# Sinkhorn gate steps, first-gate scaling and slice-pair combinations placed differently in the expert stage of one kernel

## The chip, the cores and the metric

The kernel runs on one core of a Trainium2 chip. The metric is the device time of one execution in microseconds (us). Every time below comes from runs on the chip or from one profiled execution.

## What is computed

The reference is clustered attention, then a squared-relu MLP, then a layer of eight experts whose gates are balanced by Sinkhorn iterations. Only the last part bears on the change. `x` has 1536 tokens of 512 features, `E` is 8, each expert has 1024 hidden features:

```
logits = x @ w_gate
logits = logits - logits.max()
P = exp(logits)
for _ in range(8):
    P /= P.sum(1, keepdims=True) + 1e-09      # rows: one sum per token
    P /= P.sum(0, keepdims=True) + 1e-09      # columns: one sum per expert
    P *= N / E
out = 0
for e in range(E):
    out += P[:, e:e+1] * (relu(x @ w1[e]) @ w2[e])
```

## The kernel before

**The work of the expert stage.** Tokens lie in four slices of 384 (`x1[0]` to `x1[3]`), taken as two slice pairs (0, 1) and (2, 3). The function `blocks` (line 875) runs 64 blocks, n = 0 to 63: for each slice pair the 32 weight units in turn (four units for each expert). A block multiplies x by one unit of the first expert weights in Winograd's form: seven products instead of eight, each a group of six matmuls into one PSUM tile (lines 949, 962, 976, 985, all recorded at the helper's line 120). In the text products are named by the left operand: 0, 4, 1, 5, 3, 2, 6, which is their order on TensorE. Three of them (0, 1, 6) have plain halves of x as right operand (`xh`, `xl`), the other four the combinations T1 to T4 of the two slices of the pair (`th`, `tl`). All float32 data are held in two parts.

**What stands between the products.** VectorE adds the products up (lines 952, 963, 964, 977, 978, 979, 986; ScalarE copies product 0 at line 951), relu leaves a high part `hh` on ScalarE (line 901) and a low part `hl` on VectorE (line 902), and TensorE applies the second expert weights to the relu results of the block before (`second`, line 922: nine matmuls at a time, four times per block). Each expert's result is gathered in PSUM for four blocks and then added to the output with its gate (`drain`, lines 932 and 934). ScalarE and GpSimd meanwhile split the weights of the next block in four quarters (`pieces`, lines 828 to 842), and a DMA fetches the raw unit three blocks ahead (line 807).

**PSUM.** The products of a block take turns in two PSUM buffers named `t` (`ps`, line 108, with `lanes` set to 2). A product can start when the product, or whatever else was given a buffer, two turns earlier has been read for the last time.

**The order of work** is the program's order on each engine, written out by hand; nothing is moved by a scheduler. A step that `blocks` calls between two products stands at that place in the queues of all engines that it uses.

**The gate.** `gate_steps` (line 706) makes ten steps, and with the logits of the last slice and their transposition there are twelve. From block 1 on, the helper `more` (line 939) pops one of them at two places of each block: ahead of product 3, and at the block's end. So they run in blocks 1 to 6. `gmax1` and `gmax2` find the largest logit and take the exponential; `gmax2` goes on with the first `rows`. Each `cols` step then has a matmul with a matrix of ones (line 737) that gives the column sums, four small VectorE instructions (739 to 742), a multiplication of `pm` (743), and `rows`: three small instructions (729 to 731) and another multiplication of `pm` (732). The small vectors `cs` and `rs` lie in SBUF; the PSUM tile of the matmul is last read at line 739.

**The first gate.** Expert 0's sum is drained in block 4, before the gate is known, and copied without a factor (line 932). At the end of block 6 six VectorE instructions (line 1002) scale it.

**The turn.** Block 31 is the last of the first slice pair. There, VectorE forms the T combinations of the second pair (`combine`, lines 849 to 861, ten instructions on operands in SBUF), and `parts` splits them in two (line 872 on ScalarE, 873 on GpSimd) before block 32 needs them.

Of the kernel before, what the change touches and what calls it, by code (L numbers as in the profile page):

```python
# [17 lines left out]
P = 128  # L18
# [20 lines left out]
# Per group of four heads: shifts of its preparation steps against their places.  # L39
# [14 lines left out]
class Kernel:  # L54
    """Clustered attention, a squared-relu MLP and Sinkhorn-gated experts.

    A float32 matrix product is carried by three float32r passes over the parts
    x = hi + lo, where hi is x rounded to 12 significant bits and lo the exact rest.
    """
# [7 lines left out]
    def build(self):  # L67
        tc = self.tc
        with ExitStack() as ctx:
# [7 lines left out]
            # The space of what prepares the heads goes to the first weights when it is done.  # L77
# [23 lines left out]
    def experts_follow(self):  # L101
        """The space of the first stage's weights goes to the second's."""
        self.top.__exit__(None, None, None)
        self.right.__exit__(None, None, None)
        self.right = self.tc.tile_pool(name="late", bufs=1, side="right", reuse_waits="tile")
        self.late = self.right.__enter__()
        self.top = self.tc.tile_pool(name="top2", bufs=1, reuse_waits="tile")
        self.upper = self.top.__enter__()
# [7 lines left out]
    def mm3(self, out, pairs):  # L116
        """out = sum of products of (stationary, moving) pairs."""
        n = len(pairs)
        for i, (a, b) in enumerate(pairs):
            self.nc.tensor.matmul(out, a, b, start=(i == 0), stop=(i == n - 1))  # L120

# [1 line left out]

    def constants(self):
        nc, per = self.nc, self.per
        cst = per.tile([P, 2 * P + 1], F32, name="cst")
        nc.sync.dma_start(cst, self.cst_in)
        self.ident, self.floor = cst[:, :P], cst[:, 2 * P : 2 * P + 1]
        # Its values, like the 0/1 it is multiplied with, are exact in bfloat16.
        self.band = per.tile([P, P], BF16, name="band")  # L130
        nc.vector.tensor_copy(self.band, cst[:, P : 2 * P])
# [13 lines left out]
    def centroids(self, craw):  # L145
        """Normalised centroids, transposed to [(j, d), (head, c)], as the zero-padded
        stationaries of each quadrant."""
# [10 lines left out]
        # Partition (hp, j, c) keeps its columns of half j only.  # L158
# [20 lines left out]

    def norms(self, n, soon=False):  # L180
        """Steps that give 1 / (|x| + 1e-6) for the rows of q and k."""
# [43 lines left out]
    def prepare(self, n, soon=False):  # L225
        """Steps, each with its place, that load four heads, assign clusters and build their
        stacked operands."""
# [113 lines left out]
    def attention(self):  # L341
# [123 lines left out]
        def values(half, part):  # L465
            """A third of the half head's product with v."""
# [82 lines left out]

    def load_unit(self, u):  # L550
        """Weight unit u of the first stage, in float64 words."""
# [5 lines left out]
    def words(self, u, part=None):  # L557
        """float64 to float32, first part: the high word's exponent is rebiased by a scaling, the
        low word becomes a multiple of its last bit's weight."""
# [11 lines left out]
    def bits(self, u, part=None):  # L571
        """Second part: t has the sign, the exponent and 20 fraction bits, a the power of two."""
# [9 lines left out]
    def join(self, u):  # L582
        """Third part: the low word's share is added."""
# [18 lines left out]
    def experts(self):  # L602
        nc = self.nc
        # A group of weight units is applied to each chunk of tokens in turn.
# [101 lines left out]
        def gate_steps():  # L706
            lg, pm = self.lg, self.pm
            n_t = NCH * TT
            flat = pm.rearrange("p t e -> p (t e)")

# [8 lines left out]
            def gmax2():  # L719
# [5 lines left out]
                rows()  # L725

            def rows():
                rs = self.tile("rs", [P, n_t])
# [5 lines left out]
            def cols(last):  # L734
                def run():
                    ps = self.ps("t", [P, n_t, NE])
                    nc.tensor.matmul(ps.rearrange("p t e -> p (t e)"), self.ones, flat, start=True, stop=True)
                    cs = self.tile("cs", [P, NE])
                    nc.vector.reduce_sum(cs, ps.rearrange("p t e -> p e t"), axis=AX.X)
                    nc.vector.tensor_scalar_add(cs, cs, 1e-9)  # L740
                    nc.vector.reciprocal(cs, cs)
                    nc.vector.tensor_scalar_mul(cs, cs, float(NT // NE))
                    nc.vector.tensor_tensor(pm, pm, cs.unsqueeze(1).to_broadcast([P, n_t, NE]), op=ALU.mult)
                    if not last:
                        rows()
                return run

            return [gmax1, gmax2] + [cols(i == 7) for i in range(8)]

        # The step after which each unit is split: its slot is free and its use ahead.  # L750
# [18 lines left out]
        for d, *st in (  # L769
# [3 lines left out]
            (10, self.combine, 1, 0, 0, 1), (11, self.parts, 1, 0, 1), (11, self.combine, 2, 0, 0, 1),  # L773
            (12, self.parts, 2, 0, 1), (12, self.combine, 0, 0, 0), (13, self.parts, 0, 0),
            (14, self.combine, 0, 0, 1), (14, self.combine, 3, 0, 0), (15, self.parts, 3, 0), (15, self.parts, 0, 1),
            (15, self.combine, 3, 0, 1),
# [13 lines left out]
        extra = [(logits, NCH - 1), (turn_logits, NCH - 1)] + [(st,) for st in gate_steps()]  # L790
        self.blocks(lambda i: second(n_steps - 2 + i), extra)

# [1 line left out]
    #  # L794
    # relu(x w1) is formed for two chunks of tokens and two blocks of hidden features at a time.
    # With A the blocks of w1' (hidden features by halves of the contraction) and B those of x'
    # (halves of the contraction by chunks), Winograd's form needs seven products:
    #   S1 = A21 + A22, S2 = S1 - A11, S3 = A11 - A21, S4 = A12 - S2
    #   T1 = B12 - B11, T2 = B22 - T1, T3 = B22 - B12, T4 = T2 - B21
    #   P1 = A11 B11, P2 = A12 B21, P3 = S4 B22, P4 = A22 T4, P5 = S1 T1, P6 = S2 T2, P7 = S3 T3  # L800
    #   C11 = P1 + P2, U = P1 + P6, V = U + P7, C12 = U + P5 + P3, C21 = V - P4, C22 = V + P5

    def fetch(self, k):
        """Unit k of the experts' weights: [A11 A12 A22 A21 | w2 of both blocks]."""
# [4 lines left out]
    def pieces(self, k, i):  # L809
        """The quarters of splitting unit k into A11 A12 A22 S1 S2 S3 S4 and w2."""  # L810
# [34 lines left out]
    def combine(self, i, sp, *js):  # L845
        """Halves js of T_i of slice pair sp (0 for T4)."""
        nc = self.nc
        x0, x1 = self.x1[2 * sp], self.x1[2 * sp + 1]
        sub = lambda o, a, b: nc.vector.tensor_tensor(o, a, b, op=ALU.subtract)  # L849
        for j in js:  # L850
            t = self.tile("r", [P, CH], bufs=4) if sp else self.tile("c", [P, CH], bufs=4, pool=self.late)
            self.cv[i, j] = t
# [4 lines left out]
            else:  # L857
# [3 lines left out]
                if i == 0:  # L861
                    sub(t, t, x0[:, 2 + j])

# [11 lines left out]
    def blocks(self, before, extra):  # L875
# [7 lines left out]
        def product(n, a, b):  # L883
            """a-th left operand times b, a chunk's half (c, half) or T_b."""
# [54 lines left out]
        def more():  # L939
            if extra:  # L940
                st = extra.pop(0)
                st[0](*st[1:])

        self.parts(3, 1)
        for n in range(N2):
# [12 lines left out]
            if turn:  # L958
                self.combine(2, 1, 0, 1)
                self.combine(0, 1, 0, 1)  # L960
                self.parts(2, 0, 1)
            ta, tb = product(n, 1, (c0, 1)), product(n, 5, 3)
# [8 lines left out]
            if turn:  # L971
                self.combine(3, 1, 0, 1)
                self.parts(3, 0, 1)
            if n > 0:
                more()
# [7 lines left out]
            if n > 0:  # L983
                self.pieces(n + 1, 2)
            ta = product(n, 6, (c1, 1))
# [3 lines left out]
            if turn:  # L989
                self.parts(0, 0, 1)  # L990
                self.combine(1, 1, 0, 1)
                self.parts(1, 0, 1)
            self.pieces(n + 1, 3)
            self.fetch(n + 3)
            if n > 0:
                more()
            if n == 2 * FP - 2:
                assert not extra
                for t in range(2):
                    for m in range(TT):  # L1000
                        p = self.pm[:, t * TT + m, :1]
                        nc.vector.tensor_scalar_mul(acc[t][:, m], acc[t][:, m], p)
# [10 lines left out]
def _constants():  # L1013
    """Identity; the matrix that finds the first of equal maxima; a row's floor; 1/2.

    The rows of a quadrant are (j, cluster); quadrants hold the q and k of a head pair. From the
    0/1 marks of the maxima the matrix gives 1 (k: BIG) for the first of a group and 0 or less
    for all else.
    """
# [9 lines left out]
def _layouts(inputs):  # L1029
    q, k, v = inputs["q"], inputs["k"], inputs["v"]  # L1030
    qk = np.stack([q, k])
    # [X, b, t, pair, j, s, d] -> [b, t, (pair, X), (j, d), s]
# [10 lines left out]
    # An expert's w1 [(half, kt, p), (block, fp, f)] as [fp][p][(block, half), (kt, f)], w2 [(block, fp, p), m]  # L1043
    # as [fp][p][block, m].
# [24 lines left out]
```

## Time and profile before

| | |
|---|---|
| Median of 3 timed runs | 1633.49 us (1632.96 to 1636.36) |
| Span of the profiled execution, first to last instruction | 1629.9 us |
| Own device time of the profiled execution | not listed apart; the median is 3.6 us over its span |
| TensorE busy | 1555.6 us (95%) |
| VectorE, ScalarE, GpSimd busy | 1069.4, 762.6, 888.3 us |
| Mean granted TensorE clock | 0.985 of full speed |

TensorE's matmuls are pipelined, so its busy share says only that matmuls were in flight. The stage of the experts takes the span from some 585 us to the end.

### The profile page before, as it was taken

The numbers are of one execution on the slowest core, as the hardware profiler recorded it, in microseconds if no ns is written. First come the engines' busy times: TensorE is split into PE (matmuls) and PEld (weight loads), VectorE is DVE, ScalarE is ACT, GpSimd is POOL, SyncE is SP. The second block draws the span as 40 slices with busy tenths as digits, with TensorE's granted clock in tenths as the row PEclk, the third lists the DMA queues.
The fourth block names the chain that finished last, engine by engine and source line by source line (L and its number), as shares of the span: only waits on it lengthen the run. The fifth ranks groups of instructions, "written<-read, shape, count | busy, mean of one in ns | idle before, by whom it ended". The sixth has DMA issues, their size and how long they took to land.

```text
span 1629.9 us, 21771 instructions
## 1 busy us (share of the span) xinstructions
PE 1555.6 (95%) x8136; PEld 1408.9 (86%) x8136; DVE 1069.4 (66%) x1610; ACT 762.6 (47%) x1426; POOL 888.3 (54%) x650
## 2 busy tenths in 40 slices
PE   4899998799999999989999999998999999999998
PEld 4878987699999988778989888887898898888887
DVE  7999989787887665765555555557455555555554
ACT  4789898566565643323333333333343333333331
POOL 5665337332323564546566565667566565665652
PEclk7999999899999999999999999999999999999999
DMA  9774452021111011112112121222121121211211
GB/s 269 177 189 105 88 146 79 26 74 56 55 49 52 1 52 52 52 52 78 60 70 78 52 78 53 77 78 91 52 78 69 62 78 52 78 65 65 78 53 39
DMA packets 26793, 124.69 MB, mean 77 GB/s; under 512 B 4448, under 2 KB 4576, under 8 KB 16448
## 3 DMA queue, kind: packets, MB, share of 16 engines
q1 hardware_dynamic: 26112, 120.95, 22.7%
q0 software_dynamic: 576, 2.36, 0.6%
q8 instruction: 64, 1.05, 0.3%
q14 instruction: 41, 0.34, 0.1%
HBM read 99.80 MB, written 3.15 MB: 63 GB/s over the span
## 4 chain that ended last, share of the span: by engine, by line
PE 78%; DVE 14%; ACT 4%; issue 2%; POOL 1%; DMA 1%; SPq 0%; DVEq 0%; ACTq 0%; POOLq 0%
PE t L120 31%; PE s L922 21%; PE y L922 10%; PE s L664 6%; PE pv L473 2%; PE u L120 2%; DVE atl L463 2%; PE s L422 2%; DVE m L428 2%; PE t L450 1%; DVE sums L480 1%; ACT e L435 1%; DVE hl L650 1%; DVE c L849 1%; ACT ath L457 1%
## 5 line engine op out<-in xcount | busy, mean ns | idle before, releaser
L901 ACT ACTIVATE hh<-c 128x384 fp32r<-128x384 f32 x256 | 134.5, 525 | 638.9 <-PE y L922 241.7
L902 DVE SCALAR_TENSOR_TENSOR hl<-c,hh 128x384 fp32r<-128x384 f32 x256 | 247.9, 970 | 177.3 <-ACT hh L901 177.2
L842 POOL TENSOR_TENSOR wl<-raw,wh 128x1024 fp32r<-128x1024 f32 x64 | 154.0, 2407 | 375.5 <-ACT wh L841 375.5
L922 PE MATMUL s<-wh,hh 128*128 128x512 f32 x512 | 204.7, 400 | 0.0
L922 PE MATMUL s<-wl,hh 128*128 128x512 f32 x512 | 203.6, 398 | 0.0
L922 PE MATMUL s<-wh,hl 128*128 128x512 f32 x512 | 203.0, 396 | 0.0
L120 PE MATMUL t<-th,ah 128*128 128x384 f32 x512 | 174.2, 340 | 10.6 <-DVE c L952 7.0
L834 POOL TENSOR_TENSOR al<-sm,ah 128x1024 fp32r<-128x1024 f32 x64 | 171.7, 2683 | 9.6 <-ACT ah L831 9.6
L120 PE MATMUL t<-th,al 128*128 128x384 f32 x512 | 173.4, 339 | 0.0
L120 PE MATMUL t<-tl,ah 128*128 128x384 f32 x512 | 172.9, 338 | 0.0
L120 PE MATMUL t<-xh,ah 128*128 128x384 f32 x384 | 130.7, 340 | 6.0 <-DVE c L978 3.6
L120 PE MATMUL t<-xh,al 128*128 128x384 f32 x384 | 129.7, 338 | 0.0
L120 PE MATMUL t<-xl,ah 128*128 128x384 f32 x384 | 129.4, 337 | 0.0
L963 DVE TENSOR_TENSOR c<-t,c 128x384 f32<-128x384 f32 x64 | 35.7, 557 | 136.3 <-PE t L120 136.0
L587 POOL TENSOR_TENSOR fa<-fa,wraw 128x1024 f32<-128x1024 f32 x16 | 39.1, 2445 | 150.9 <-ACT r L646 107.9
L832 POOL TENSOR_TENSOR al<-raw,ah 128x768 fp32r<-128x768 f32 x64 | 118.8, 1856 | 0.0
L922 PEld LDWEIGHTS s<-wh,hl 128*128 128x128 f32 x512 | 97.2, 190 | 24.2
L120 PEld LDWEIGHTS t<-th,ah 128*128 128x128 f32 x512 | 96.5, 189 | 16.8 <-DVE c L952 7.9
L922 PEld LDWEIGHTS s<-wh,hh 128*128 128x128 f32 x512 | 97.0, 189 | 12.0
L922 PEld LDWEIGHTS s<-wl,hh 128*128 128x128 f32 x512 | 96.9, 189 | 12.0
L922 PE MATMUL y<-wh,hl 128*128 128x512 f32 x256 | 100.9, 394 | 0.0
L922 PE MATMUL y<-wl,hh 128*128 128x512 f32 x256 | 100.9, 394 | 0.0
(218 smaller groups left out, 4093.6 us busy)
## 6 DMA issues: line engine op xcount, KB each, us to landing
raw<-in_w SPq DMA_DIRECT2D x64, 1024.0 KB, 4.8
wraw<-in_w SPq DMA_DIRECT2D x16, 1024.0 KB, 4.8
raw<-in_qk SPq DMA_DIRECT2D x16, 384.0 KB, 4.2
ka<-hi SPq DMA_DIRECT2D x28, 192.0 KB, 3.7
nat<-in_qkn SPq DMA_DIRECT2D x6, 768.0 KB, 5.2
vraw<-in_v SPq DMA_DIRECT2D x8, 384.0 KB, 4.5
out<-x SPq DMA_DIRECT2D x12, 256.0 KB, 2.1
qa<-hi SPq DMA_DIRECT2D x14, 192.0 KB, 2.6
```

Source lines behind the costliest of these rows:

```text
L120: self.nc.tensor.matmul(out, a, b, start=(i == 0), stop=(i == n - 1))
L422: nc.tensor.matmul(s[:, u, :HALF], a[:, qs], k[:, u * HALF : u * HALF + HALF], start=(a is qa), stop=(a is qb))
L428: nc.vector.tensor_reduce(m, sc[g][:, :, :HALF], axis=AX.XY, op=ALU.max, negate=True)
L587: nc.gpsimd.tensor_tensor(a, a, raw[:, :, 0].bitcast(F32), op=ALU.mult)
L664: nc.tensor.matmul(o, a, b, start=(start and i == 0), stop=(stop and i == 2))
L832: nc.gpsimd.tensor_tensor(al[:, : 3 * Q], raw[:, : 3 * Q], f32(ah[:, : 3 * Q]), op=ALU.subtract)
L834: nc.gpsimd.tensor_tensor(al[:, 3 * Q :], self.sums.rearrange("p a b -> p (a b)"), f32(ah[:, 3 * Q :]), op=ALU.subtract)
L842: nc.gpsimd.tensor_tensor(wl, raw[:, 1024:], f32(wh), op=ALU.subtract)
L901: nc.scalar.activation(hh, c, AF.Relu)
L902: nc.vector.scalar_tensor_tensor(hl, c, 0.0, f32(hh), op0=ALU.max, op1=ALU.subtract)
L922: nc.tensor.matmul(ys[t][m], a, b, start=(start and i == 0), stop=(stop and i == 2))
L963: nc.vector.tensor_tensor(p1, ta, p1, op=ALU.add)
```

## The change

Three edits, all in the expert stage.

1. The Sinkhorn steps. `rows` and `total` (the old `cols`) are now 16 single steps; with the logits, their transposition, `gmax1` and `gmax2` there are 20. `more` is called at four places of a block instead of two (ahead of product 1, of product 3, of product 6, and at the end), so the steps run in blocks 1 to 5. The vectors `rs` and `cs` lie in PSUM, `rs` in a `t` buffer of its own and `cs` beside the column sums in theirs. One instruction is left out per column step: the addition and the multiplication by the constant are one.
2. The first-gate scaling is six multiplications on ScalarE instead of VectorE, two at each of the first three places of block 7.
3. The combinations of the second slice pair are eight VectorE instructions instead of ten, each reading two operands in SBUF, one at each place of blocks 29 and 30; T1 and T4 overwrite parts of `x1` in place. Block 31 keeps only the splitting, T1's ahead of product 6.

```diff
         def gate_steps():
...
-                rows()
+
+            def total():
+                ps = hold["ps"] = self.ps("t", [P, n_t + 1, NE])
+                nc.tensor.matmul(
+                    ps[:, :n_t].rearrange("p t e -> p (t e)"), self.ones, flat, start=True, stop=True
+                )
+                cs = ps[:, n_t]
+                nc.vector.reduce_sum(cs, ps[:, :n_t].rearrange("p t e -> p e t"), axis=AX.X)
+                nc.vector.tensor_scalar(cs, cs, 1e-9, float(NE / NT), op0=ALU.add, op1=ALU.mult)
+                nc.vector.reciprocal(cs, cs)
+                nc.vector.tensor_tensor(pm, pm, cs.unsqueeze(1).to_broadcast([P, n_t, NE]), op=ALU.mult)
 
             def rows():
-                rs = self.tile("rs", [P, n_t])
+                rs = self.ps("t", [P, n_t])
...
-            def cols(last):
...
-            return [gmax1, gmax2] + [cols(i == 7) for i in range(8)]
+            def first_gate(t, m):
+                a = self.flat[t].rearrange("p (m n) -> p m n", n=512)[:, m]
+                nc.scalar.mul(a, a, pm[:, t * TT + m, :1])
+
+            steps = [(gmax1,), (gmax2,)] + [(rows,), (total,)] * 8
+            return steps, [(first_gate, t, m) for t in range(2) for m in range(TT)]
...
+    def next_combine(self, i, j):
+        nc = self.nc
+        x0, x1 = self.x1[2], self.x1[3]
+        t = {1: x1[:, j], 0: x0[:, 2 + j]}.get(i)
+        if t is None:
+            t = self.tile("r", [P, CH], bufs=4)
+        self.cv[i, j] = t
+        a, b, op = {
+            3: (x1[:, 2 + j], x1[:, j], ALU.subtract), 2: (self.cv.get((3, j)), x0[:, j], ALU.add),
+            1: (x1[:, j], x0[:, j], ALU.subtract), 0: (self.cv.get((2, j)), x0[:, 2 + j], ALU.subtract),
+        }[i]
+        nc.vector.tensor_tensor(t, a, b, op=op)
...
-        def more():
-            if extra:
+        ahead = [(self.next_combine, i, j) for i in (3, 2, 1, 0) for j in range(2)]
+
+        def more(n):
+            if 0 < n < U2 and extra:
                 st = extra.pop(0)
+                st[0](*st[1:])
+            elif n == 2 * FP - 1 and scales:
+                for st in scales[:2]:
+                    st[0](*st[1:])
+                del scales[:2]
+            elif U2 - 3 <= n < U2 and ahead:
+                st = ahead.pop(0)
                 st[0](*st[1:])
...
             if turn:
-                self.combine(2, 1, 0, 1)
-                self.combine(0, 1, 0, 1)
                 self.parts(2, 0, 1)
+            more(n)
             ta, tb = product(n, 1, (c0, 1)), product(n, 5, 3)
...
             if turn:
-                self.combine(3, 1, 0, 1)
                 self.parts(3, 0, 1)
-            if n > 0:
-                more()
+            more(n)
             ta, tb = product(n, 3, 1), product(n, 2, 0)
...
+            if turn:
+                self.parts(1, 0, 1)
+            more(n)
             ta = product(n, 6, (c1, 1))
...
             if turn:
                 self.parts(0, 0, 1)
-                self.combine(1, 1, 0, 1)
-                self.parts(1, 0, 1)
             self.pieces(n + 1, 3)
             self.fetch(n + 3)
-            if n > 0:
-                more()
-            if n == 2 * FP - 2:
-                assert not extra
-                for t in range(2):
-                    for m in range(TT):
-                        p = self.pm[:, t * TT + m, :1]
-                        nc.vector.tensor_scalar_mul(acc[t][:, m], acc[t][:, m], p)
+            more(n)
```

## Rows read from the trace of the kernel before

**Rows 1.** The page's head and its part 1, busy time by engine.

```profile
span 1629.9 us, 21771 instructions
...
PE 1555.6 (95%) x8136; PEld 1408.9 (86%) x8136; DVE 1069.4 (66%) x1610; ACT 762.6 (47%) x1426; POOL 888.3 (54%) x650
```

**Rows 2.** Busy time by stretch; bounds are starts of a block's first product.

```profile
core 0: us, PE busy (x) PEld busy (x) DVE busy (x) ACT busy (x) POOL busy (x), PEclk, DMA share, GB/s
597.37:615.85 18.48, 17.69 (x91) 14.83 (x90) 7.99 (x14) 6.11 (x11) 10.79 (x8) 1.00 0.16 58
615.85:632.68 16.83, 16.46 (x83) 14.25 (x81) 7.60 (x14) 5.36 (x10) 9.71 (x7) 1.00 0.15 62
597.37:730.17 132.80, 121.01 (x578) 104.13 (x577) 85.05 (x162) 40.68 (x71) 68.75 (x50) 0.96 0.15 56
706.63:730.17 23.54, 18.55 (x82) 15.98 (x80) 16.37 (x22) 5.10 (x9) 9.86 (x7) 0.85 0.12 45
730.17:1091.56 361.39, 361.39 (x1795) 324.39 (x1794) 197.23 (x289) 121.83 (x207) 223.49 (x161) 1.00 0.18 68
1091.56:1130.16 38.60, 34.02 (x158) 29.27 (x156) 29.17 (x35) 14.29 (x26) 29.58 (x22) 0.96 0.20 76
```

**Rows 3.** Waits of TensorE from 600 to 720 us: total, times, longest.

```profile
PE t L120 <- DVE c L952: 7.0, 3, 5.0
PE t L120 <- DVE c L978: 3.6, 3, 1.8
```

**Rows 4.** Single lines: duration in ns (least, median, most), first and last start, shape.

```profile
L742 DVE TENSOR_SCALAR cs<-cs x8: 171/1129/2305, 644.0 to 708.3; 128x8 f32<-128x8 f32 x8
...
L1002 DVE TENSOR_SCALAR x<-x,pm x6: 474/942/2018, 711.4 to 716.3; 128x512 f32<-128x512 f32 x6
...
L963 DVE TENSOR_TENSOR c<-t,c x64: 543/557/559, 590.9 to 1607.0; 128x384 f32<-128x384 f32 x64
...
L739 DVE TENSOR_REDUCE cs<-t x8: 249/255/258, 641.6 to 707.5; 128x8 f32<-128x96 f32 x8
...
L729 DVE TENSOR_REDUCE rs<-pm x8: 252/253/253, 634.2 to 701.2; 128x12 f32<-128x96 f32 x8
...
L737 PEld LDWEIGHTS t<-pm,ones x16: 187/188/189, 641.0 to 706.5; 128*128 128x128 f32 x16
```

**Rows 5.** Timeline over the end of block 4 and the start of block 5.

```profile
668.74 0.35 PE L737 MATMUL t<-pm,ones 128*128 128x96 f32 x2
...
668.87 0.42 PE L120 MATMUL t<-xh,ah 128*128 128x384 f32 x1
...
669.79 0.25 DVE L739 TENSOR_REDUCE cs<-t 128x8 f32<-128x96 f32 x1
...
670.18 0.42 PE L120 MATMUL t<-th,ah 128*128 128x384 f32 x1
...
671.77 0.26 DVE L732 TENSOR_TENSOR pm<-pm,rs 128x96 f32<-128x96 f32 x1
```

**Rows 6.** Timeline of block 1 where product 6 starts.

```profile
612.35 0.33 PE L120 MATMUL t<-xh,ah 128*128 128x384 f32 x1
...
612.88 0.56 DVE L902 SCALAR_TENSOR_TENSOR hl<-c,hh 128x384 fp32r<-128x384 f32 x1 [1.39 <-ACT hh L901]
```

**Rows 7.** Timeline of block 30, VectorE and GpSimd after product 5.

```profile
1082.83 2.20 DVE L902 SCALAR_TENSOR_TENSOR hl<-c,hh 128x384 fp32r<-128x384 f32 x1
...
1084.58 2.72 POOL L834 TENSOR_TENSOR al<-sm,ah 128x1024 fp32r<-128x1024 f32 x1
1085.51 0.56 DVE L977 TENSOR_TENSOR c<-t,c 128x384 f32<-128x384 f32 x1 [0.48 <-PE t L120]
```

**Rows 8.** Timeline across the end of block 31 and the start of block 32.

```profile
1112.28 4.54 POOL L873 TENSOR_TENSOR tl<-r,th 128x384 fp32r<-128x384 f32 x4 [2.01 <-ACT th L872]
1112.31 2.70 DVE L849 TENSOR_TENSOR r<-x,x 128x384 f32<-128x384 f32 x2
...
1116.49 0.47 ACT L951 COPY c<-t 128x384 f32<-128x384 f32 x1
...
1117.02 0.45 PE L120 MATMUL t<-xh,ah 128*128 128x384 f32 x1 [2.30 <-ACT c L951]
```

**Rows 9.** Line 932, ScalarE's scaled copies of 128x512.

```profile
L932 ACT ACTIVATE x<-s,pm x4: 668/679/687, 1185.2 to 1194.0; 128x512 f32<-128x512 f32 x4
```

More of the change, by code (lines that the diff above doesn't have):

```diff
@@ L709, in gate_steps @@
             flat = pm.rearrange("p t e -> p (t e)")
+            hold = {}
             def gmax1():
@@ L732, in rows @@
                 nc.vector.tensor_tensor(pm, pm, rs.unsqueeze(2).to_broadcast([P, n_t, NE]), op=ALU.mult)
-            def cols(last):
[L735 to L746, printed above, removed]
-            return [gmax1, gmax2] + [cols(i == 7) for i in range(8)]
+            def first_gate(t, m):
[3 more added lines that the diff above has]
+            return steps, [(first_gate, t, m) for t in range(2) for m in range(TT)]
         plan = {}
@@ L772, in experts @@
             (10, pieces, 1, 2), (14, pieces, 0, 3), (15, self.fetch, 2),
[L773 to L776, printed above, removed]
+            (10, self.combine, 1, 0, 1), (11, self.parts, 1, 0, 1), (11, self.combine, 2, 0, 1),
+            (12, self.parts, 2, 0, 1), (12, self.combine, 0, 0), (13, self.parts, 0, 0),
+            (14, self.combine, 0, 1), (14, self.combine, 3, 0), (15, self.parts, 3, 0), (15, self.parts, 0, 1),
+            (15, self.combine, 3, 1),
         ):
@@ L789, in experts @@
                 st[0](*st[1:])
-        extra = [(logits, NCH - 1), (turn_logits, NCH - 1)] + [(st,) for st in gate_steps()]
-        self.blocks(lambda i: second(n_steps - 2 + i), extra)
+        gates, scales = gate_steps()
+        self.blocks(lambda i: second(n_steps - 2 + i), [(logits, NCH - 1), (turn_logits, NCH - 1)] + gates, scales)
     def fetch(self, k):
@@ L843, in pieces, with combine @@
             self.raws.pop(U1 + k)
-    def combine(self, i, sp, *js):
+    def combine(self, i, *js):
         nc = self.nc
-        x0, x1 = self.x1[2 * sp], self.x1[2 * sp + 1]
+        x0, x1 = self.x1[0], self.x1[1]
         sub = lambda o, a, b: nc.vector.tensor_tensor(o, a, b, op=ALU.subtract)
         for j in js:
-            t = self.tile("r", [P, CH], bufs=4) if sp else self.tile("c", [P, CH], bufs=4, pool=self.late)
-            self.cv[i, j] = t
+            t = self.cv[i, j] = self.tile("c", [P, CH], bufs=4, pool=self.late)
             if i == 1:
@@ L873, in parts, with blocks @@
             nc.gpsimd.tensor_tensor(tl[:, i, j], t, f32(th[:, i, j]), op=ALU.subtract)
-    def blocks(self, before, extra):
+    def blocks(self, before, extra, scales):
         nc = self.nc
@@ L990, in blocks @@
                 self.parts(0, 0, 1)
-                self.combine(1, 1, 0, 1)
-                self.parts(1, 0, 1)
             self.pieces(n + 1, 3)
             self.fetch(n + 3)
-            if n > 0:
-                more()
-            if n == 2 * FP - 2:
-                assert not extra
-                for t in range(2):
-                    for m in range(TT):
-                        p = self.pm[:, t * TT + m, :1]
-                        nc.vector.tensor_scalar_mul(acc[t][:, m], acc[t][:, m], p)
+            more(n)
+            assert n < 2 * FP or not extra + scales
         second(N2 - 1, 0, 0)
```

## The prediction

> **What bounds the kernel now.** I began with the page's engine shares: TensorE is busy for 1555.6 of 1629.9 us, 95% [rows 1]. That says where the bound is, not where time is lost, so next I cut the expert stage into stretches at the starts of its blocks. The 23 blocks from 730.17 to 1091.56 take 361.39 us, TensorE busy in all of it, at full granted clock: 15.71 us per block [rows 2]. No small edit on another engine can shorten these. Two stretches are longer than their blocks. Blocks 1 to 7, which hold the gate, take 132.80 us, 22.8 more than 7 x 15.71. Blocks 31 and 32, the turn, take 38.60, 7.2 more than 2 x 15.71 [rows 2]. These 30.0 us are all that the three edits can reach.
>
> Then I asked who keeps TensorE waiting in the gate stretch: VectorE's additions at lines 952 and 978, 10.6 us in six waits [rows 3]. They aren't slow; line 963, an addition of the same kind, takes 557 ns whatever else runs [rows 4]. They stand behind gate instructions in VectorE's queue, and some of these last far too long: line 742 works on eight columns and takes 171 ns at best, 1129 at the median, 2305 at most [rows 4]. Line 739, which reads PSUM, never takes over 258, and line 963, which reads PSUM too, never over 559. So what waits is an instruction with all its operands in SBUF; long GpSimd instructions run beside them, and one VectorE instruction of 0.56 us ended just behind such a one (2.20 us, from 1082.83, beside GpSimd's work up to 1084.58) [rows 6, 7]. I take it that an operand in PSUM spares the wait.
>
> **The change part by part.** The sum is made against the profiled span, 1629.9; the median of the runs, 1633.5, is 3.6 above it, and I carry that over.
>
> *First-gate scaling.* Removed: six instructions at line 1002, 474 to 2018 ns each [rows 4], right ahead of block 7's first addition. The stretch from 706.63 is 23.54 us, 7.8 over a block, at a granted clock of 0.85 on average [rows 2]: the wait, and the slower matmuls after it. Added: six ScalarE multiplications of 128x512 in block 7, nearest row 679 ns [rows 9], 1.4 us per place. ScalarE is busy for 121.83 us in 23 blocks, 5.3 of 15.7 [rows 2], and the relus queued behind the pair feed a second layer that runs a block later. Cost 0 to 1.4 us if that cover were gone; I take 0. Block 7 loses its 7.8.
>
> *Sinkhorn steps.* Eight matmuls with ones stay eight. Each loads weights twice at 188 ns, 0.38 at most [rows 4]; the next product starts 0.13 after it [rows 5]. I take the middle, 0.25: 2.0 us for eight.
>
> Block 1 now also gets `gmax1`, ahead of product 6. Its reduction stands on VectorE behind the second `hl` of the pair, which ran from 612.88 to 613.44, and TensorE was ready for product 6 at 612.35 [rows 6]. With a reduction of 0.25 (line 729) [rows 4] and a hand-over of 0.14 (below) TensorE waits until 613.83, 1.5 us. Block 1's own surplus, 18.48 - 15.71 = 2.8 [rows 2], stays (logits, their transposition and a wait for block 0). Block 2's surplus, 16.83 - 15.71 = 1.1 [rows 2], holds both gmax steps' work, and moves up; 0.4 of it I count as their old wait, an estimate. Block 1: 2.8 + 1.5 + 0.7 = 5.0.
>
> In blocks 2 to 5 a column step ends each block. Its tile is a `t` buffer, and product 4 of the next block needs that. Before, the buffer was free after line 739: it ran from 669.79 to 670.04, and product 4 began at 670.18, 0.14 later and 1.31 after product 0 [rows 5]. Now the buffer is held through the last multiplication. Nine instructions took from 669.79 to 672.03, 0.25 each [rows 5], so a step of four takes 1.0, the release comes 0.75 later, and product 4 starts 2.06 after product 0 instead of about 1.06: 1.0 us of waiting, four times (blocks 3 to 6), 4.0.
>
> The column step ahead of product 3 holds the buffer of product 2. It starts behind the `hl` that ended at 1085.03; the addition of product 3's result began at 1085.51 [rows 7], some 1.2 after that product began, so product 2 is due near 1085.4 and the buffer is free at 1085.03 + 1.0 + 0.14 = 1086.2. That is 0.8 in block 2; in blocks 3 to 5 TensorE is already a microsecond behind GpSimd's timetable, and I leave 0.2 each: 1.4. The row steps hold buffers that are due more than 2 us later: 0.
>
> Gate after: 5.0 + 2.0 + 4.0 + 1.4 = 12.4. Before: 22.8. Gain 10.4. With all waits hidden that could overlap it would be near 8 left (gain 15); with every step half a microsecond later, near 20 (gain 3).
>
> [...] The same 96 values are reduced in 255 ns from PSUM (line 739) and in 253 from SBUF (line 729) [rows 4], so I charge nothing. [...]
>
> *Combinations ahead.* Block 31 loses ten VectorE instructions. The last two, 2.70 us from 1112.31, held up ScalarE's splitting and behind it the copy of product 0 at 1116.49, for which TensorE waited 2.3 us [rows 8]. Blocks 29 and 30 get eight, one per place, still reading SBUF alone. A step behind the `hl` that ended at 1085.03 finds GpSimd at line 834 until 1084.58 + 2.72 = 1087.30 [rows 7]; it ends near 1087.9, where the additions of products 3 and 2 had begun at 1085.51. Two additions of 0.56 later the buffer that product 6 needs is free, near 1089.0; product 6 is due 21 of a block's 78 matmuls, 4.2 us, after product 3, near 1088.5. So it is 0.5 late. Twice: 1.1. The other places have over 1 us of room. Splitting remains: GpSimd's four low parts took 4.54 us [rows 8], eight take 9.1 beside its 223.49 / 23 = 9.7 per block [rows 2], 28.5 of 31.4 us in two blocks; I add 0.4. Turn after: 1.5, between 0 and all of the 7.2. Gain 5.7.
>
> No DMA is added; the fetch stands ahead of the fourth place as before, so SP's queue is passed by nothing.
>
> **Sum.** 10.4 + 5.7 = 16.1; span 1629.9 - 16.1 = 1613.8, time 1633.5 - 16.1 = **1617.4 us**.
>
> **The rivals.**
> *The turn gives nothing.* GpSimd's splitting is what ends last, as its near-full 28.5 us suggests; against it, TensorE's wait named ScalarE's copy [rows 8]. Gain 10.4: 1623.1.
> *An operand in PSUM doesn't spare the wait.* Then the eight column steps free their buffers about 1.1 later (line 742's median less its least is 0.96, and other instructions wait too): 8.8 of the gate's gain goes, time 1626.2. For it: no row shows an instruction from PSUM to PSUM. Against it: lines 739 and 963.
> *Slower: the product buffers.* Each of 16 steps now takes one of two `t` buffers until VectorE has finished it. If TensorE waits w for every one, the gate takes 5.0 + 2.0 + 16w, and this is slower than before once 16w exceeds 22.8 + 5.7 - 7.0 = 21.5, w over 1.3 us. At line 742's 2.3 it gives 1633.5 + 16 x 2.3 - 21.5 = 1648.8. Against it: a step lasts 1.0, and half of them are due late.
> *More gain.* Waits for product 4 overlap others: 1612.
>
> **How the numbers follow.** My forecast gets 0.75, the turn rival 0.09, the PSUM rival 0.08, the slower one 0.04, more gain 0.04. The range 1612 to 1625 takes in forecast, turn rival and the bounds of the unknown waits, and leaves out the PSUM rival and the slower one. A measurement can tell some 0.2% from no change, 3.3 us (the runs shown spread over 3.4). Faster by more than that: 0.93; within: 0.03; slower: 0.04.
>
> **What the next profile would show.** Right: the stretch of the gate blocks near 122 us and of the turn near 33; no small gate instruction over 0.4 us; product 4 some 2 us after product 0 in blocks 3 to 6; no half-clock stretch in block 7. Wrong: small vectors in PSUM still lasting 1 to 2 us, TensorE waiting for row steps too, ScalarE's copy of product 0 late in block 7, or a turn still near 38.

## The result, and the profile after

The changed kernel takes 1611.6 us (1610.82 to 1614.97, 4 runs) beside 1633.22 of the kernel before: a ratio of 0.9866 with a 95% interval of 0.9848 to 0.9885, 21.6 us less. The forecast was 1617.4 with a range from 1612: right in direction, but the gain was 5.5 us larger than forecast, and the time fell just outside the range, 0.4 us below it.

The page's head and part 1 of the changed kernel, which answer to [rows 1]:

```profile
span 1609.0 us, 21766 instructions
...
PE 1544.8 (96%) x8136; PEld 1402.2 (87%) x8136; DVE 1009.2 (63%) x1594; ACT 766.4 (48%) x1432; POOL 892.3 (55%) x650
```

Busy time by stretch, columns as in [rows 2]: blocks 1 to 7, blocks 8 to 30, the turn, then block 8 and block 9 alone:

```profile
597.98:719.46 121.48, 116.42 (x577) 101.04 (x577) 62.37 (x148) 44.35 (x77) 68.92 (x50) 1.00 0.17 61
719.46:1079.76 360.30, 360.30 (x1795) 323.96 (x1794) 189.35 (x296) 121.83 (x207) 226.01 (x161) 1.00 0.19 68
1079.76:1111.09 31.33, 31.33 (x158) 28.16 (x156) 17.57 (x26) 13.78 (x26) 28.66 (x22) 1.00 0.26 93
719.46:735.16 15.70, 15.70 (x79) 14.13 (x78) 9.32 (x14) 5.29 (x9) 9.74 (x7) 1.00 0.18 67
735.16:750.78 15.62, 15.62 (x79) 14.04 (x78) 8.07 (x14) 5.30 (x9) 9.81 (x7) 1.00 0.19 68
```

The spans differ by 20.9 us. Blocks 1 to 7 gave 132.80 - 121.48 = 11.3, the turn 38.60 - 31.33 = 7.3. These were expected. Not expected: blocks 8 to 30, which no edit touches, take 360.30 instead of 361.39, because odd blocks now last 15.62 us; over blocks 8 to 30 and 33 to the end that is 2.9. Block 1 starts 0.6 later. No block from block 1 on has a stretch at a granted clock of 0.50 any more, half of the full clock; the kernel before had three, in blocks 5, 7 and 32 (684.9 to 688.3, 715.6 to 722.4 and 1118.4 to 1121.8).

Waits of TensorE from 597 to 720 us, against [rows 3]:

```profile
PE t L120 <- ACT c L977: 1.9, 3, 0.6
PE t L717 <- DVE gm L715: 1.1, 1, 1.1
PE t L120 <- DVE c L1012: 0.8, 1, 0.8
PE t L120 <- DVE pm L737: 0.8, 1, 0.8
```

And small gate instructions by line, against [rows 4]; line 735 is the column step's, 742 the row step's, 748 the first-gate scaling:

```profile
L735 DVE TENSOR_SCALAR t<-t x8: 174/174/175, 627.6 to 688.3; 128x8 f32<-128x8 f32 x8
L742 DVE TENSOR_SCALAR t<-t x8: 178/178/179, 621.6 to 685.1; 128x12 f32<-128x12 f32 x8
L744 DVE TENSOR_TENSOR pm<-pm,t x8: 253/254/254, 622.1 to 685.6; 128x96 f32<-128x96 f32 x8
L748 ACT ACTIVATE x<-x,pm x6: 709/711/722, 706.4 to 717.3; 128x512 f32<-128x512 f32 x6
```

No small instruction waits any more, and the waits left are 4.6 us instead of 10.6. So the trace seems to bear the forecast out, with the steady blocks as the only open point. The experiments say otherwise on two more: what made the gate faster, and how much of the turn's 7.3 us was waiting.

### The profile page after: what moved, and what is told of

The parts are those of the page before. It is cut to its first block, busy times and chain, and to the rows that moved or that the text cites. A ratio compares the mean times of both kernels' runs of the same rounds, so it can differ in the third digit from the quotient of the medians.

```text
span 1609.0 us, 21766 instructions
## 1 busy us (share of the span) xinstructions
PE 1544.8 (96%) x8136; PEld 1402.2 (87%) x8136; DVE 1009.2 (63%) x1594; ACT 766.4 (48%) x1432; POOL 892.3 (55%) x650
## 4 chain that ended last, share of the span: by engine, by line
PE 81%; DVE 9%; ACT 4%; issue 2%; DMA 2%; POOL 1%; SPq 0%; DVEq 0%; ACTq 0%; POOLq 0%
PE t L120 33%; PE s L938 22%; PE y L938 11%; PE s L664 6%; PE pv L473 3%; PE u L120 2%; PE s L422 2%; DVE atl L463 2%; DVE m L428 2%; PE t L450 1%; DVE sums L480 1%; ACT e L435 1%; DVE hl L650 1%; DVE c L852 1%; PE u L450 1%
## 5 line engine op out<-in xcount | busy, mean ns | idle before, releaser
L918 DVE SCALAR_TENSOR_TENSOR hl<-c,hh 128x384 fp32r<-128x384 f32 x256 | 211.9, 829 | 170.9 <-ACT hh L917 170.9
L938 PE MATMUL s<-wh,hh 128*128 128x512 f32 x512 | 200.9, 392 | 0.0
L837 POOL TENSOR_TENSOR al<-sm,ah 128x1024 fp32r<-128x1024 f32 x64 | 165.7, 2589 | 4.9 <-ACT ah L834 4.9
L835 POOL TENSOR_TENSOR al<-raw,ah 128x768 fp32r<-128x768 f32 x64 | 129.7, 2027 | 0.0
L938 PEld LDWEIGHTS s<-wl,hh 128*128 128x128 f32 x512 | 96.0, 188 | 11.8
```

The source lines that it names most:

```text
L835: nc.gpsimd.tensor_tensor(al[:, : 3 * Q], raw[:, : 3 * Q], f32(ah[:, : 3 * Q]), op=ALU.subtract)
L837: nc.gpsimd.tensor_tensor(al[:, 3 * Q :], self.sums.rearrange("p a b -> p (a b)"), f32(ah[:, 3 * Q :]), op=ALU.subtract)
L918: nc.vector.scalar_tensor_tensor(hl, c, 0.0, f32(hh), op0=ALU.max, op1=ALU.subtract)
L938: nc.tensor.matmul(ys[t][m], a, b, start=(start and i == 0), stop=(stop and i == 2))
```

## The experiments

In the built programs one thing differs that the steady blocks use: with `rs` and `cs` gone from SBUF, the tiles allocated behind them, the odd units' first weights `ah1` and `al1`, start 96 bytes lower, at byte 144544 of each partition instead of 144640. Two runs move only that.

**x1_pad.** The place is filled up again.

```diff
-                neg = self.tile("gneg", [P, 1])
+                neg = self.tile("gneg", [P, 25])[:, :1]
```

> The changed kernel with 96 bytes of unused space per partition put back where the two small vectors lay, so that the odd units' first weights (ah1, al1) start at byte 144640 again, as before the change, instead of 144544. Nothing else changes. Theory (the steady blocks gained because these weights moved): the odd blocks take 15.72 us again instead of 15.62, 28 of them after the gate and some in it, so the time rises by 2.5 to 3.2 us to about 1614.5, with gate and turn as in the changed kernel. Rival (the steady blocks gained from the order of work, the turn of the product buffers or the queues): nothing changes, 1611.6, odd blocks at 15.62.

Measured: 1615.52 us (6 runs), ratio 0.9897 (0.9878 to 0.9915). Blocks 1 to 7, block 8 and block 9 of this run:

```profile
602.23:724.02 121.79, 116.74 (x578) 101.14 (x578) 63.86 (x148) 44.34 (x77) 68.76 (x50) 1.00 0.17 61
724.02:739.72 15.70, 15.70 (x80) 14.13 (x78) 9.30 (x14) 5.29 (x9) 9.70 (x7) 1.00 0.18 67
739.72:755.44 15.72, 15.72 (x79) 14.08 (x78) 9.61 (x14) 5.30 (x9) 9.76 (x7) 1.00 0.18 68
```

Block 9 is back at 15.72, the gate stretch within 0.3. The median is 3.9 us above the changed kernel's, about 3 of it from the blocks. The profiled execution, the slowest of the six at 1618.16 us, is no measure of the rest: its block 1 began 4 us later than the changed kernel's.

**x2_shift.** The kernel before, with its vectors in an existing buffer.

```diff
-                rs = self.tile("rs", [P, n_t])
+                rs = self.tile("r", [P, CH], bufs=4)[:, :n_t]
...
-                    cs = self.tile("cs", [P, NE])
+                    cs = self.tile("r", [P, CH], bufs=4)[:, :NE]
```

> The kernel before with the two small vectors put into an existing SBUF buffer (the tag r), so that the odd units' first weights start at byte 144544, as in the changed kernel; order of work and placement in SBUF as before. Theory (place of the weights): odd blocks 15.62 instead of 15.72, time lower by 2.5 to 3.2 us, about 1630.3, with gate near 22.8 and turn near 7.2 over their blocks. Rival: same as before, 1633.2.

Measured: 1628.21 us beside 1631.88, ratio 0.9975 (0.9964 to 0.9987). Its gate stretch took 132.85, as before, and its block 9 is as in the changed kernel:

```profile
746.65:762.27 15.62, 15.62 (x79) 14.04 (x78) 8.07 (x14) 5.30 (x9) 9.81 (x7) 1.00 0.19 69
```

The turn was 1.6 shorter too, which I didn't expect and which isn't the weights' doing: x4_psum and x6_scale below, with the weights at their old place, have it as well (37.06 us). Both runs: the steady gain is the place of the odd weights.

**x7_late.** Would the even ones gain too? A tile of 64 bytes that nothing uses moves `ah0` and `al0` from 180192 to 180128, and the raw units by as much.

```diff
+            if k == 0:
+                self.tile("lpad", [P, 16], pool=self.late)
             sm = self.sums = self.tile("sm", [P, 4, Q], pool=self.late)
```

> The changed kernel with the even units' first weights (ah0, al0) and the raw units moved down by 64 bytes per partition, from 180192 to 180128, nothing else. The odd units' weights gave 15.62 us per odd block at 144544 (32 above a multiple of 128) and 15.72 at 144640 (a multiple of 128); the even ones lie 96 above one. Theory A (the pace goes by the place within 128 bytes, and 32 is the good one): even blocks fall from 15.70 to about 15.62, time 2 to 3 us less than 1611.6. Theory B (it goes by something else, such as which other tiles are read beside them): even blocks at 15.70 or slower.

Measured: 1609.26 us, ratio 0.9853 (0.9836 to 0.987). Blocks 8 and 9:

```profile
718.55:734.16 15.61, 15.61 (x79) 14.04 (x78) 9.34 (x14) 5.29 (x9) 9.74 (x7) 1.00 0.18 67
734.16:749.77 15.61, 15.61 (x79) 14.04 (x78) 9.74 (x14) 5.30 (x9) 9.76 (x7) 1.00 0.18 68
```

**x11_64.** The same with the odd weights at 144576 (`gneg` of 9 columns).

> The kernel of x7_late with the odd units' first weights at byte 144576, 64 above a multiple of 128, instead of 32 above one; one look for the blocks' pace. Theory A (only 32 above a multiple of 128 is good): odd blocks slower than 15.65. Theory A2 (the pace is lost only at or next to a multiple of 128, at 0 and 96): odd blocks at 15.61 to 15.62. The time itself differs by at most 3 us and is not read.

Measured, blocks 8 and 9 of a single execution:

```profile
719.08:734.70 15.62, 15.62 (x80) 14.04 (x79) 9.34 (x14) 5.30 (x9) 9.74 (x7) 1.00 0.20 67
734.70:750.42 15.72, 15.72 (x80) 14.16 (x79) 9.55 (x14) 5.29 (x9) 9.74 (x7) 1.00 0.21 68
```

Of the four places within 128 bytes that were tried, 32 gave 15.61 to 15.62 (two addresses), 0, 64 and 96 gave 15.70 to 15.72. Theory A stands for these; why 32 is good was not tried. By the starts of the matmuls in the traces it isn't simply that the weights of a badly placed unit load slowly: at 144640 some 0.08 of the 0.10 us lost per block falls on the second-layer matmuls behind products 4 and 5, whose own operands haven't moved, while at 180192 the loss falls on the products themselves: in block 8 of the changed kernel two products took 2.11 us, in block 9, at 144544, 2.08.

**x3_sbuf.** Single steps kept, vectors back in SBUF, addresses unmoved.

```diff
-                cs = ps[:, n_t]
+                cs = self.tile("r", [P, CH], bufs=4)[:, :NE]
...
-                rs = self.ps("t", [P, n_t])
+                rs = self.tile("r", [P, CH], bufs=4)[:, :n_t]
```

> The changed kernel, its 20 single steps at four places kept, but the small vectors in SBUF (the tag r, so no address moves) instead of PSUM. Theory (an operand in PSUM spares the wait beside GpSimd): small instructions of 1 to 2.3 us come back, the column steps end later, blocks 1 to 7 go from 11.5 to some 18 to 22 us over their 7 x 15.7, time about 1619 to 1623. Rival (the shorter steps at four places are what helped): gate within 2 us of the changed kernel's, time 1611 to 1613.

Measured: 1608.56 us (4 runs), ratio 0.9855 (0.9835 to 0.9875): not slower than the changed kernel but 3 us faster, below both forecasts. The ratios' intervals overlap, so what counts is the gate stretch. Blocks 1 to 7 as a stretch, the column step's lines, and the start of block 4 on the timeline:

```profile
599.39:717.56 118.17, 115.55 (x578) 101.03 (x578) 78.90 (x148) 44.58 (x77) 69.24 (x50) 1.00 0.18 63
...
L735 DVE TENSOR_SCALAR r<-r x8: 170/172/2045, 629.0 to 687.1; 128x8 f32<-128x8 f32 x8
...
L737 DVE TENSOR_TENSOR pm<-pm,r x8: 257/1219/2403, 631.2 to 687.5; 128x96 f32<-128x96 f32 x8
```

```profile
652.27 0.42 PE L120 MATMUL t<-xh,ah 128*128 128x384 f32 x1
...
653.19 0.25 DVE L734 TENSOR_REDUCE r<-t 128x8 f32<-128x96 f32 x1
...
653.58 0.41 PE L120 MATMUL t<-th,ah 128*128 128x384 f32 x1
...
653.91 2.40 DVE L737 TENSOR_TENSOR pm<-pm,r 128x96 f32<-128x96 f32 x1
```

The waits of 2 us are back, as the theory had it, and cost little: product 4 started at 653.58, 0.14 after the reduction, while the multiplication behind it took 2.40. Only in block 5, where two instructions of one step waited, did TensorE lose 0.65 us behind line 1001. The same place as above in the changed kernel, where the column step still holds its buffer and product 4 has to wait for ScalarE's copy of product 0 (line 977) to free the other:

```profile
652.21 0.42 PE L120 MATMUL t<-xh,ah 128*128 128x384 f32 x1
...
653.13 0.26 DVE L734 TENSOR_REDUCE t<-t 128x8 f32<-128x96 f32 x1
...
653.61 0.48 ACT L977 COPY c<-t 128x384 f32<-128x384 f32 x1
...
653.88 0.25 DVE L737 TENSOR_TENSOR pm<-pm,t 128x96 f32<-128x96 f32 x1
...
654.14 0.44 PE L120 MATMUL t<-th,ah 128*128 128x384 f32 x1 [0.62 <-ACT c L977]
```

The vectors in PSUM thus cost 121.48 - 118.17 = 3.3 us. In blocks 3 to 6 product 4 starts 1.31 us after product 0 here, and 1.91 to 2.07 in the changed kernel; that is 2.6 of it.

**x4_psum.** The kernel before with only the vectors in PSUM (and `gneg` widened as in x1_pad).

```diff
-                rs = self.tile("rs", [P, n_t])
+                rs = self.ps("t", [P, n_t])
...
-                    ps = self.ps("t", [P, n_t, NE])
+                    ps = self.ps("t", [P, n_t + 1, NE])
...
-                    cs = self.tile("cs", [P, NE])
+                    cs = ps[:, n_t]
```

> The kernel before with only the small vectors moved to PSUM (row sums in a t buffer of their own, column vectors beside the column sums), the long steps at two places kept, the weights left at their old addresses. Theory (the wait goes, but each long step of nine instructions, 2.2 us, now holds product buffers to its end): the small instructions fall to 0.15 to 0.3 us, blocks 3 to 6 still wait about 1.5 to 2.5 us each, blocks 1 to 7 18 to 22 us over, time 1628 to 1632. Rival (PSUM alone was the gain of the gate): blocks 3 to 6 at most 1 us over each, time 1624 to 1626. Second rival (buffers held longer cost more than the waits did): slower than 1633.

Measured: 1638.36 us, ratio 1.0036 (1.002 to 1.0053): the second rival. A line and a wait of this run:

```profile
L743 DVE TENSOR_TENSOR pm<-pm,t x8: 253/254/254, 647.5 to 717.4; 128x96 f32<-128x96 f32 x8
...
PE t L120 <- DVE pm L743: 11.8, 7, 2.1
```

No instruction waits, and the products wait 11.8 us for a column step to give its buffer back.

**x6_scale.** Only the second edit.

```diff
+        def scale(n, k):
+            if n == 2 * FP - 1 and k < 3:
+                for t, m in [(t, m) for t in range(2) for m in range(TT)][2 * k : 2 * k + 2]:
+                    nc.scalar.mul(acc[t][:, m], acc[t][:, m], self.pm[:, t * TT + m, :1])
...
-                        nc.vector.tensor_scalar_mul(acc[t][:, m], acc[t][:, m], p)
```

> The kernel before with only the second edit: the six first-gate multiplications on ScalarE in block 7, two at each of three places. Theory (they stood ahead of block 7's first additions on VectorE, and the long wait lowered the granted clock): block 7 falls from 7.8 us over a block to at most 2 (the last gate step still ends late), no stretch at half clock after it; 6 to 8 us less than before, about 1625. Rival (the last gate step is what delays block 7): at most 4 us less, above 1628.

Measured: 1621.6 us beside 1632.46, ratio 0.9936 (0.9913 to 0.9958). Blocks 1 to 7, block 5 and block 7:

```profile
599.47:723.34 123.87, 117.04 (x578) 101.04 (x577) 79.20 (x156) 44.57 (x77) 68.69 (x50) 1.00 0.17 60
671.01:689.56 18.55, 16.70 (x85) 14.43 (x84) 12.39 (x29) 6.75 (x13) 9.77 (x7) 1.00 0.18 57
707.27:723.34 16.07, 16.05 (x82) 14.12 (x80) 10.53 (x16) 8.96 (x15) 9.74 (x7) 1.00 0.19 66
```

Block 7 falls from 23.54 to 16.07: 7.5 us from this edit. Block 5 has the same work and waits as before but takes 18.55 us, not 20.11: there the granted clock stayed at full level in this execution, and so it did in the turn (below). The medians differ by 10.9 us, more than the 6 to 8 forecast; the clock in these two places, some 3 us, would make up the difference.

**x5_turn.** Only the third edit: `next_combine` as in the change's diff, called one at a time in blocks 29 and 30, and the old calls of `combine` in block 31 left out.

> The kernel before with only the third edit: the second pair's combinations as eight single instructions in blocks 29 and 30, the splitting as in the changed kernel. Theory: blocks 31 and 32 fall from 7.2 us over two blocks to 0, blocks 29 and 30 stay at 15.7, the clock stays at full level there; 7 us less than before, about 1625. Rival (GpSimd's eight low parts end last): blocks 31 and 32 still 3 us or more over, time above 1628.

Measured: 1627.0 us beside 1632.46, ratio 0.9962 (0.9949 to 0.9976). Blocks 8 to 30 and the turn:

```profile
733.17:1094.57 361.40, 361.40 (x1796) 324.39 (x1795) 203.26 (x296) 121.86 (x207) 224.77 (x161) 1.00 0.19 68
1094.57:1125.99 31.42, 31.42 (x157) 28.21 (x156) 17.90 (x26) 13.78 (x26) 28.35 (x22) 1.00 0.26 93
```

Two plain blocks, to a hundredth; the rival falls. The medians differ by 5.5 us, not the 7 forecast; the part on the turn below says why that may be.

**x9_two.** x3_sbuf with two steps at each of two places.

```diff
             if 0 < n < U2 and extra:
-                st = extra.pop(0)
-                st[0](*st[1:])
+                for _ in range(1 if n == 1 else 2 if self.place % 2 == 0 else 0):
+                    st = extra.pop(0)
+                    st[0](*st[1:])
```

> The changed kernel with the small vectors in SBUF as in the run x3_sbuf (1608.6 us, blocks 1 to 7 8.2 us over), but from block 2 on two steps at a time at the two old places, instead of one at each of four. The work is the same. Theory (what helped the gate is the spacing: a single step of four instructions, even with one of 2 us among them, fits between the additions that TensorE waits for): blocks 2 to 6 wait 2 us and more each again, blocks 1 to 7 14 to 18 us over, time 1615 to 1619. Rival (spacing doesn't matter, the scaling and the turn are the whole gain): within 2 us of 1608.6.

Measured: 1638.32 us, ratio 1.0036 (1.0023 to 1.0049), far over the forecast. TensorE's largest wait in it (21.0 us in seven times):

```profile
PE t L730 <- DVE pm L744: 21.0, 7, 4.0
```

The pairs came as row step, column step, so the column matmul waits in TensorE's queue for the row step just issued; the old pairs were the other way round. Spacing matters, but this run overstates how much. The cleaner measure is x6_scale against x3_sbuf: the same scaling and vectors in SBUF, long steps 123.87, single steps 118.17, 5.7 us apart. Up to 0.4 of that is the place of the odd weights, which differs between the two (four odd blocks). No run separates the shorter steps, the two further places and the instruction left out per column step.

**x8_best.** x3_sbuf and x7_late together, and both gmax steps two places later.

```diff
-            steps = [(gmax1,), (gmax2,)] + [(rows,), (total,)] * 8
+            steps = [(lambda: None,)] * 2 + [(gmax1,), (gmax2,)] + [(rows,), (total,)] * 8
```

> What the runs so far point to, together: the changed kernel with the small vectors in SBUF (as in x3_sbuf), both gmax steps two places later, so that the first stands ahead of product 1 of block 2, where VectorE is free 1 us before TensorE needs it, and the even weights 64 bytes lower (as in x7_late). Theory: blocks 1 to 7 from 8.2 us over to about 6.5 (the wait of 1.1 us for the first gmax step goes), all steady blocks at 15.61, time 1604 to 1606. Rival (the row and column steps, now half a block later, meet GpSimd's long instructions at worse points): blocks 3 to 7 over by 3 us more, time 1607 to 1609.

Measured: 1602.58 us (5 runs) beside 1636.25, ratio 0.9801 (0.9774 to 0.9828), better than both kernels. Blocks 1 to 7 and 8 to 30:

```profile
598.55:715.23 116.68, 115.16 (x578) 100.78 (x578) 80.83 (x148) 44.68 (x77) 69.28 (x50) 1.00 0.19 64
715.23:1074.33 359.10, 359.10 (x1795) 322.88 (x1794) 180.74 (x296) 121.78 (x207) 227.21 (x161) 1.00 0.20 68
```

The gate is 116.68 - 109.97 = 6.7 us over seven blocks of 15.71, forecast 6.5, and the steady blocks are at 15.61. The time is 1.4 us below the forecast, beside a kernel before that was 3 to 4 us slower than in the earlier comparisons.

## Why the prediction was right or wrong

**The step that failed** is the first: that no small edit on another engine can shorten the steady blocks, and that 30.0 us were all that the edits could reach. The rows showed only that TensorE never idles there; I took its pace as given. It wasn't: the edits moved the odd units' first weights by 96 bytes, and the odd blocks fell from 15.72 to 15.62 us. That came to 2.9 us, and without it the time would have been some 1614.5, inside the range. x1_pad and x2_shift show the cause. Of the rest of the 5.5 us, the turn gave 1.6 more than forecast and the gate 0.9.

**First-gate scaling.** 7.8 us forecast for block 7; 7.5 in x6_scale. The multiplications took 711 ns, not 679, and nothing waited for them.

**Sinkhorn steps.** 12.4 us over seven blocks forecast, 11.5 measured. The parts: block 1 took 20.38 of the forecast 20.7; product 4 started 1.91 to 2.07 us after product 0 in blocks 3 to 6, forecast 2.06. The size was right, the waiting partner not quite: the buffer was held by the column step, as forecast, but in the built program product 4 then gets the buffer of product 0 and waits for ScalarE's copy, which ends at about the same time (654.09 and 654.13 in the rows above). So a built program doesn't hand out its buffers strictly in turns.

**What the forecast credited wrongly.** An operand in PSUM does spare the wait beside GpSimd (253 to 255 ns against up to 2403 for the same multiplication), and that saved next to nothing: single steps leave enough room that all but 0.65 us of the waits are hidden, while the held buffers cost 3.3 us. The mechanism of the third rival (slower: the product buffers), a buffer held to the end of a step, is real; on the long steps it made the kernel slower by 0.36% (x4_psum), on the single ones it only cut the gain. From before to after the gate's 11.3 us are, by the stretches of single executions and to 0.2 us: scaling 7.5, the half-clock stretch of block 5, gone, about 1.6, single steps 5.7 (the weights' place included), vectors in PSUM -3.3.

The reading behind it, that an instruction with all its operands in SBUF waits, was too wide, and its own rows said so: line 729 reduces from SBUF to SBUF and never took over 253 ns. In block 3 of the kernel before it ran beside a GpSimd instruction, and the next one, a scalar addition, waited for that one's end:

```profile
633.94 2.40 POOL L842 TENSOR_TENSOR wl<-raw,wh 128x1024 fp32r<-128x1024 f32 x1 [7.03 <-ACT wh L841]
...
634.17 0.25 DVE L729 TENSOR_REDUCE rs<-pm 128x12 f32<-128x96 f32 x1 [0.68 <-ACT pm L724]
...
634.46 1.91 DVE L730 TENSOR_SCALAR rs<-rs 128x12 f32<-128x12 f32 x1
```

Reciprocals never waited either (202 or 203 ns for all eight at line 736 of x3_sbuf; in the kernel before, line 741 took 0.20 us at 679.40, beside GpSimd's 2.40 us from 679.29). Those that did are the scalar instructions and those on two tensors, among them the multiplications (line 732 of the kernel before, 257 to 2227 ns), the combinations (line 849, 544 to 2745) and `hl` (543 to 2757).

The prediction charged nothing for small vectors in PSUM. Apart from the waits, the runs agree, to 13 ns an instruction. In the changed kernel and in x3_sbuf the scalar instruction on 12 columns took 178 ns in PSUM and 174 (median) in SBUF, that on eight 174 and 172, and the largest difference, of the reciprocals, was 13 ns (241 and 228, 216 and 203).

**The turn.** The term was mis-sized: 1.5 us forecast, 0 measured. I let each ahead step wait for GpSimd's second long instruction, because block 30 showed `hl` waiting out the first. In the changed kernel `hl` slipped in ahead of the first, and the step waited for that one alone; in block 29 the additions began at 1058.19 with room left, and block 30 went the same way:

```profile
1055.35 0.79 DVE L918 SCALAR_TENSOR_TENSOR hl<-c,hh 128x384 fp32r<-128x384 f32 x1
1055.69 2.16 POOL L835 TENSOR_TENSOR al<-raw,ah 128x768 fp32r<-128x768 f32 x1
...
1056.07 2.20 DVE L878 TENSOR_TENSOR r<-x 128x384 f32<-128x384 f32 x1
1057.81 2.73 POOL L837 TENSOR_TENSOR al<-sm,ah 128x1024 fp32r<-128x1024 f32 x1
1058.19 0.55 DVE L1000 TENSOR_TENSOR c<-t,c 128x384 f32<-128x384 f32 x1
```

The 7.2 us that I took for the turn were those of one execution, and 1.5 of them weren't waiting. Block 32 held a stretch at a granted clock of 0.50 there; in x6_scale, with the same work and the same waits in the turn (2.3, 1.7 and 0.5 us), it stayed at 1.00. Block 32 in the kernel before, the stretch in it, then block 32 in x6_scale:

```profile
1109.61:1130.16 20.55, 17.76 (x80) 15.35 (x78) 13.12 (x18) 7.15 (x13) 14.83 (x12) 0.92 0.25 91
1118.40:1121.80 3.40, 3.40 (x11) 3.03 (x10) 2.14 (x3) 0.52 (x1) 3.32 (x5) 0.50 0.48 140
...
1102.78:1121.79 19.01, 16.25 (x79) 14.02 (x78) 12.63 (x18) 7.07 (x13) 15.30 (x12) 1.00 0.28 98
```

The turn as a whole took 37.06 in x6_scale and in x4_psum, 5.6 over two blocks, which fits the 5.5 us that x5_turn gained in its medians.

## What to carry to other kernels

Where an engine is the bound, small instructions on another engine matter by where they stand and by which buffer they hold to the end: put them singly into gaps, and let a product buffer's last read come as early as it can. An edit that takes away a tile can move the tiles behind it (here by 96 bytes, 15.62 us per odd block instead of 15.72); compare the pace of stretches that the edit doesn't touch before crediting it with the whole difference. A stretch taken from one execution can hold time lost to a lower clock that another execution doesn't lose (here 20.11 us beside 18.55): look at the clock before counting it as waiting. A wait in the trace is worth removing only if the step behind it is late without it: take it away alone, in the new order, and measure.

## What the hardware showed unexpectedly

TensorE's pace depends on where the stationary weights start: 15.61 to 15.62 us for a block of 78 matmuls (42 of them with these weights) with weights at byte 144544 or 180128, 15.70 to 15.72 at 144576, 144640 or 180192, with TensorE busy throughout at full granted clock.

The granted clock falls after similar waits in some executions and not in others: block 5 of the kernel before held a stretch at 0.50 and took 20.11 us (x2_shift and x5_turn, with the same gate steps: 20.12 and 20.11), while the same block in x6_scale, with the same steps and the same wait of 1.8 us, stayed at 1.00 and took 18.55. Block 5 of the kernel before, and the stretch in it:

```profile
668.87:688.98 20.11, 18.26 (x85) 15.68 (x84) 12.47 (x29) 6.75 (x13) 9.78 (x7) 0.92 0.14 53
...
684.90:688.30 3.40, 3.40 (x10) 2.84 (x9) 1.14 (x3) 0.18 (x1) 0.00 (x0) 0.50 0.00 0
```
